# Pinning the matmul order of a Sinkhorn mixture of experts, spreading the Sinkhorn calls, and keeping two Strassen sums in PSUM

## The chip, the core and the metric

The kernel runs on one core of a Trainium2 chip. The metric is the device time of one execution in microseconds (us). The profile names the engines PE (TensorE, matmuls; PEld is its weight load), DVE (VectorE), ACT (ScalarE), POOL (GpSimd) and SP (SyncE, which issues the DMAs). PSUM is the memory that TensorE writes its results to; the kernel uses it in eight banks.

## The reference

A banded attention feeds a dense mixture of experts. The attention has 4 batches, 8 heads, 768 positions and 64 columns a head; a position sees 8 global positions and the last 96. Its output, as x of 3072 tokens by 512 columns, goes through all 8 experts, and the experts' outputs are mixed with weights P that a Sinkhorn iteration balances:

```python
logits = x @ w_gate
P = np.exp(logits - logits.max())
for _ in range(8):
    P /= P.sum(1, keepdims=True) + 1e-09
    P /= P.sum(0, keepdims=True) + 1e-09
    P *= N / E
for e in range(E):                       # w1[e]: 512 x 1024, w2[e]: 1024 x 512
    h = np.maximum(x @ w1[e], 0.0)
    out += P[:, e:e + 1] * (h @ w2[e])
```

Everything is float32.

## The kernel before

Each float32 operand of the mixture is split into a high and a low part (`hh`/`hl`, `w2h`/`w2l` and so on), and a product takes three matmuls: high by low, low by high, high by high.

The first 350 us or so are the attention, with part of expert 0 computed in its gaps (the filler). There the matmuls go through the class `InOrder`, which pins each of them behind the one traced before it on TensorE. After the attention, `moe.pe = nc.tensor` lifts the pinning. The last filler, the last gate and all of the mixture then run in whatever order the planner chose. The planner orders each engine's instructions ahead of time with a simulated timeline of its own; on the chip each engine works through its list in that order.

The mixture is a list of 120 steps, `steps`, in two halves of 60. A step is a pair of 128-column blocks of hidden units of one expert (`g`) for 768 tokens (`b`). Two neighbouring steps mostly share the weights of one `g` and take the two token blocks of the half. A step has two parts:

- The first layer, `layer1_strassen` (L641 on): x times w1 for two blocks by two, as seven Strassen products of six matmuls each, 42 in all, each 384 columns wide. The products accumulate in four PSUM banks, `c`, `d`, `a`, `b`, in the order m3 (c), m2 (d), m1 (a), m6 (b), m5 (c), m4 (d), m7 (a). ACT copies bank c to `t3` after m3 (L657); DVE forms the other sums (L659 to L670) in the two SBUF tiles `t3` and `h22`. `relu_split` then makes `hh` on ACT (L624) and `hl` on DVE (L625) from `h22`, `c`, `d` and `t3`. There are four such banks (`mps`), so each step uses the banks of the step before again.
- The second layer, `second`: six output tiles `y_ps` of 128 tokens, each of six matmuls 512 columns wide (L684 to L686), 36 in all, in three PSUM buffers (`yps`). DVE evicts each tile into the accumulator `acc`, times a column of P (L936); for expert 0, which is not scaled yet, it only adds (L932). At the first tiles of expert 1, ACT scales what expert 0 left in `acc` (L935).

The trace of the program goes: first layer of step n, weight split for the next g (`strassen_pair`: casts on ACT at L536, differences on POOL at L537), second layer of step n - 1.

P is computed by the generator `sinkhorn`, which `second` advances with `next`. It takes eleven calls: the first two find the maximum, the third takes exp and the first row sums, each later one does a matmul with ones for the column sums (`c_ps`, L747), the column division (L749 to L753) and, except in the last, the next row division (L741 to L744). With three calls a second layer it ends within the first four, all of which belong to expert 0.

Of the kernel before, what the change touches and what calls it, by code (L numbers as in the profile page):

```python
# [12 lines left out]
ALU = mybir.AluOpType  # L13
# [480 lines left out]
class Moe:  # L494
# [146 lines left out]
    def layer1_strassen(self, x, w, hpool, tmp, ps, tag):  # L641

        nc, KH = self.nc, self.KH
        wh, wl = w[0:2]
        left = {"m1": 0, "m2": 1, "m3": 5, "m4": 6, "m5": 2, "m6": 3, "m7": 4}
        bank = {n: ps.tile([P, UNIT], F32, name=f"bank_{n}", tag=tag) for n in "cdab"}

        def product(m, n, first, last):
            i, (xh, xl) = left[m], x[m]
            self.products(bank[n], lambda c: wh[:, i, c], lambda c: wl[:, i, c], lambda c: xh[:, c],  # L650
                          lambda c: xl[:, c], KH, first, last)

        a, b, c, d = (bank[n] for n in "abcd")
        tt = nc.vector.tensor_tensor
        product("m3", "c", True, False)
        t3 = tmp.tile([P, UNIT], F32, name="t3")
        nc.scalar.copy(out=t3, in_=c)  # L657
        product("m2", "d", True, False)
        tt(out=t3, in0=t3, in1=d, op=ALU.subtract)  # L659
        product("m1", "a", True, False)  # L660
        h22 = tmp.tile([P, UNIT], F32, name="h22")
        tt(out=h22, in0=a, in1=t3, op=ALU.add)
        product("m6", "b", True, True)
        tt(out=h22, in0=b, in1=h22, op=ALU.add)  # L664
        product("m5", "c", False, True)
        product("m4", "d", False, True)
        tt(out=t3, in0=d, in1=t3, op=ALU.add)
        tt(out=t3, in0=t3, in1=c, op=ALU.subtract)
        product("m7", "a", False, True)
        tt(out=t3, in0=a, in1=t3, op=ALU.add)  # L670
        r22 = self.relu_split(h22, hpool)
        r12 = self.relu_split(c, hpool)
        r21 = self.relu_split(d, hpool)
        r11 = self.relu_split(t3, hpool)
        return [r11, r21], [r12, r22]

    def layer2(self, t, w, hs, ps, tag):
# [78 lines left out]
def pipeline(tc, attention, ident, moe, acc):  # L756
# [6 lines left out]
    with ExitStack() as top:  # L763
# [72 lines left out]
        def differences(b, units=(0, 1)):  # L836
            for i in units:
                moe.right_difference(ops[b], i, xtmp, b == NB - 1)
            spill_blocks(b, ((0, KH), (1, 0)))
            settled.add(b)  # L840
# [49 lines left out]
        hpool = top.enter_context(tc.tile_pool(name="hpool", bufs=8, reuse_waits="tile"))  # L890
        tmp = top.enter_context(tc.tile_pool(name="ctmp", bufs=2, reuse_waits="tile"))

        def reload(b, pool):
            xs[2 * b], xs[2 * b + 1] = x_tiles(), x_tiles()
            new = [(pool.tile([P, KH, UNIT], F32R, name=f"sh{n}"), pool.tile([P, KH, UNIT], F32R, name=f"sl{n}"))
                   for n in range(3)]
            for i in range(2):
                for s in range(2):
                    nc.sync.dma_start(out=xs[2 * b + i][s].bitcast(F32), in_=x_spill[b][i][s].bitcast(F32))
            for i in range(3):  # L900
                for s in range(2):
                    nc.sync.dma_start(out=new[i][s].bitcast(F32), in_=s_spill[b][i][s].bitcast(F32))
            (h0, l0), (h1, l1) = xs[2 * b], xs[2 * b + 1]
            ops[b] = {"m1": new[0], "m2": (h0[:, 0:KH], l0[:, 0:KH]), "m3": (h1[:, 0:KH], l1[:, 0:KH]),
                      "m4": (h0[:, KH:], l0[:, KH:]), "m5": (h1[:, KH:], l1[:, KH:]), "m6": new[1], "m7": new[2]}
# [10 lines left out]
        def seed(b):  # L916
            for i in range(2):
                if 2 * b + i < NU - 1:
                    nc.sync.dma_start(out=acc_of[b][:, i * UT:(i + 1) * UT], in_=y_spill[2 * b + i])

        def second(g, b, hs):
            e = groups[g % NG][0]
            first_scaled = e != 0 and groups[g % NG - 1][0] == 0
            for i in range(2):
                for t in range(UT):
                    tt = (2 * b + i) * UT + t
                    y_ps = moe.layer2(t, wts[g], hs[i], yps, "y")
                    if t == 0 or i * t == 2:
                        next(sinkhorn, None)
                    a = acc_of[b][:, i * UT + t]  # L930
                    if e == 0:
                        nc.vector.tensor_tensor(out=a, in0=y_ps, in1=a, op=ALU.add)  # L932
                    else:
                        if first_scaled:
                            nc.scalar.mul(a, a, moe.pm[:, tt, 0:1])  # L935
                        nc.vector.scalar_tensor_tensor(out=a, in0=y_ps, scalar=moe.pm[:, tt, e:e + 1], in1=a,  # L936
                                                       op0=ALU.mult, op1=ALU.add)
                    if g % NG == NG - 1:
                        nc.sync.dma_start(out=moe.out[tt * P:(tt + 1) * P, :], in_=a)
# [2 lines left out]
            seed(b)  # L942
        sinkhorn = moe.sinkhorn(sps, "s")
        prev = None
        for n, (g, b) in enumerate(steps):
            hs = moe.layer1_strassen(ops[b], wts[g], hpool, tmp, mps, "h")
            if n == 0:
                with tc.issue_after(moe.latest.ins):
                    differences(NB - 1)
            for p, bs in enumerate(halves[:-1]):  # L950
                if b in bs and n == last_use[b]:
                    reload(halves[p + 1][bs.index(b)], sums[bs.index(b)])
            if g + 1 < 2 * NG and g + 1 not in wts:
                wts[g + 1] = moe.strassen_pair(moe.strassen_stage(*groups[(g + 1) % NG], stage), wpools[(g + 1) % 2])
            if prev is not None:
                second(*prev)
                for p, bs in enumerate(halves[:-1]):
                    if prev[1] in bs and n - 1 == last_use[prev[1]]:
                        seed(halves[p + 1][bs.index(prev[1])])
            prev = (g, b, hs)  # L960
        second(*prev)


@with_exitstack
def kernel(
# [31 lines left out]
    with tc.If(rv > 0) as cmp:  # L997
        pipeline(tc, band, ident, moe, acc)
    with cmp.Else():
        pipeline(tc, Dense(tc, q, k, v, ng, nl), ident, moe, acc)  # L1000
# [32 lines left out]
```

## Time and profile before

| | |
|---|---|
| time of three runs | 2261.06, 2262.77, 2263.44 us (median 2262.77) |
| the profiled execution's own time | 2260.31 us |
| its span, first to last instruction | 2258.5 us |
| granted TensorE clock | 0.996 of full |
| PE / DVE / ACT / POOL busy | 98% / 66% / 32% / 36% of the span |
| first mixture step starts | 368.9 us |

The profiled execution's time is its span and 1.8 us around it, and it lies 2.5 us under the median. Matmuls are pipelined: a matmul's row in the timeline shows a duration of 0.33 or 0.39 us, but the next one starts after about half of that, so it is the distance between starts that counts, and a TensorE that is "100% busy" can still be slower or faster. In a row of a group the numbers behind the bar are the busy time in us, the mean of one in ns, the idle time of the engine before it and what ended that.

### The profile page before, as it was taken

What the parts mean: (1) busy time and instruction counts of PE and PEld (TensorE: products, weight loads), DVE (VectorE), ACT (ScalarE), POOL (GpSimd) and SP (SyncE); (2) the same over time, 40 slices, a digit from 0 to 9 for tenths busy, and PEclk for the clock granted to TensorE, in tenths of its full rate; (3) what the DMA queues carried; (4) which work ended last, traced back from release to release, by engine and by line L of the source; (5) the groups of instructions that cost most, each with busy time, mean ns of one, the idle gap of its engine ahead of it and who ended that gap; (6) DMA issues with size and microseconds to landing.
All of it is one profiled execution on the core that took longest, in us unless ns stands there. A gap on an engine that the chain in (4) does not pass through costs nothing.

```text
span 2258.5 us, 31464 instructions
## 1 busy us (share of the span) xinstructions
PE 2224.2 (98%) x12147; PEld 1981.0 (88%) x12147; DVE 1501.7 (66%) x2682; ACT 712.9 (32%) x1592; POOL 819.5 (36%) x655
## 2 busy tenths in 40 slices
PE   7999999999999999999999999999999999999998
PEld 5788888989899898998999989989899898998997
DVE  5555457876666676666766666676676666766665
ACT  5676663232222222222222133222222222222221
POOL 4166366333333333333333234333333333333320
PEclk8999999999999999999999999999999999999999
DMA  6465432011100111001110451101111010111101
GB/s 167 121 178 160 127 102 66 29 38 38 38 28 29 38 38 38 28 29 38 38 38 29 166 206 39 38 29 34 32 38 38 29 38 29 38 38 31 36 19 58
DMA packets 177615, 133.74 MB, mean 59 GB/s; under 512 B 117041, under 2 KB 148785, under 8 KB 177457
## 3 DMA queue, kind: packets, MB, share of 16 engines
q1 hardware_dynamic: 177456, 131.65, 19.3%
q8 instruction: 97, 1.59, 0.3%
q14 instruction: 62, 0.50, 0.1%
HBM read 108.81 MB, written 22.81 MB: 58 GB/s over the span
## 4 chain that ended last, share of the span: by engine, by line
PE 91%; ACT 3%; DVE 2%; issue 2%; POOL 1%; DMA 0%; SPq 0%; ACTq 0%; DVEq 0%; POOLq 0%
PE y_ps L685 15%; PE y_ps L686 15%; PE y_ps L684 15%; PE bank_d L617 4%; PE bank_d L616 4%; PE bank_c L616 4%; PE bank_c L618 4%; PE bank_a L617 4%; PE bank_c L617 4%; PE bank_d L618 4%; PE bank_a L616 4%; PE bank_a L618 4%; PE bank_b L616 2%; PE bank_b L618 2%; PE bank_b L617 2%
## 5 line engine op out<-in xcount | busy, mean ns | idle before, releaser
L936 DVE SCALAR_TENSOR_TENSOR acc<-y_ps,pm,acc 128x512 f32<-128x512 f32 x672 | 499.9, 747 | 327.3 <-PE y_ps L686 324.7
L686 PE MATMUL y_ps<-w2h,hh 128*128 128x512 f32 x1440 | 567.5, 394 | 0.0
L685 PE MATMUL y_ps<-w2h,hl 128*128 128x512 f32 x1440 | 566.9, 394 | 0.0
L684 PE MATMUL y_ps<-w2l,hh 128*128 128x512 f32 x1440 | 561.8, 390 | 0.0
L537 POOL TENSOR_TENSOR w2l<-w2f,w2h 128x1024 fp32r<-128x1024 f32 x60 | 144.7, 2412 | 700.5 <-ACT w2h L536 700.5
L686 PEld LDWEIGHTS y_ps<-w2h,hh 128*128 128x128 f32 x1440 | 270.1, 188 | 53.7
L684 PEld LDWEIGHTS y_ps<-w2l,hh 128*128 128x128 f32 x1440 | 270.4, 188 | 43.5 <-DVE acc L936 0.2
L685 PEld LDWEIGHTS y_ps<-w2h,hl 128*128 128x128 f32 x1440 | 270.0, 188 | 43.4
L559 POOL TENSOR_TENSOR wsum<-w1f 128x256 f32<-128x256 f32 x300 | 223.6, 781 | 219.1 <-DMA w1f<-in_moe_w_dram 219.1
L537 POOL TENSOR_TENSOR wl<-wsum,wh 128x1280 fp32r<-128x1280 f32 x60 | 177.6, 2959 | 281.1 <-ACT wh L536 281.1
L624 ACT ACTIVATE hh<-h 128x384 fp32r<-128x384 f32 x120 | 63.1, 526 | 501.1 <-DVE h L664 499.6
L625 DVE SCALAR_TENSOR_TENSOR hl<-t,hh 128x384 fp32r<-128x384 f32 x120 | 165.4, 1378 | 9.9 <-ACT hh L624 9.8
L616 PE MATMUL bank_c<-xl,wh 128*128 128x384 f32 x480 | 162.0, 337 | 1.6 <-ACT t L657 1.6
L616 PE MATMUL bank_d<-xl,wh 128*128 128x384 f32 x480 | 160.9, 335 | 1.7 <-DVE t L670 1.7
L618 PE MATMUL bank_c<-xh,wh 128*128 128x384 f32 x480 | 161.9, 337 | 0.0
L617 PE MATMUL bank_c<-xh,wl 128*128 128x384 f32 x480 | 161.2, 336 | 0.0
L617 PE MATMUL bank_d<-xh,wl 128*128 128x384 f32 x480 | 161.2, 336 | 0.0
L617 PE MATMUL bank_a<-sh,wl 128*128 128x384 f32 x480 | 161.1, 336 | 0.0
L616 PE MATMUL bank_a<-sl,wh 128*128 128x384 f32 x480 | 161.0, 336 | 0.0
L618 PE MATMUL bank_a<-sh,wh 128*128 128x384 f32 x480 | 160.8, 335 | 0.0
L618 PE MATMUL bank_d<-xh,wh 128*128 128x384 f32 x480 | 160.3, 334 | 0.0
L625 DVE SCALAR_TENSOR_TENSOR hl<-h,hh 128x384 fp32r<-128x384 f32 x120 | 111.2, 927 | 68.7 <-ACT hh L624 68.7
(195 smaller groups left out, 3891.7 us busy)
## 6 DMA issues: line engine op xcount, KB each, us to landing
w1f<-in_moe_w_dram SPq DMA_DIRECT2D x62, 512.0 KB, 3.4
w2f<-in_moe_w_dram SPq DMA_DIRECT2D x62, 512.0 KB, 3.7
out_dram<-acc SPq DMA_DIRECT2D x24, 256.0 KB, 2.2
ys<-y_sb SPq DMA_DIRECT2D x21, 256.0 KB, 2.6
acc<-ys SPq DMA_DIRECT2D x7, 768.0 KB, 4.4
acc<-in_q_dram SPq DMA_DIRECT2D x32, 96.0 KB, 2.7
acc<-in_k_dram SPq DMA_DIRECT2D x32, 96.0 KB, 2.6
acc<-in_v_dram SPq DMA_DIRECT2D x32, 96.0 KB, 2.2
```

What stands on the lines that cost most here:

```text
L537: self.nc.gpsimd.tensor_tensor(out=lo, in0=full, in1=hi, op=ALU.subtract)
L559: nc.gpsimd.tensor_tensor(out=s[:, n], in0=x, in1=y, op=op)
L616: self.pe.matmul(out, lhsT=hi(c), rhs=xlo(c), start=(first and c == 0), stop=False, skip_group_check=True)
L617: self.pe.matmul(out, lhsT=lo(c), rhs=xhi(c), start=False, stop=False, skip_group_check=True)
L618: self.pe.matmul(out, lhsT=hi(c), rhs=xhi(c), start=False, stop=(last and c == n - 1), skip_group_check=True)
L624: nc.scalar.activation(out=hh, in_=src, func=AF.Relu)
L625: self.latest = nc.vector.scalar_tensor_tensor(out=hl, in0=src, scalar=0.0, in1=hh, op0=ALU.max, op1=ALU.subtract)
L684: self.pe.matmul(y_ps, lhsT=hh[:, cols], rhs=lf, start=(f == 0), stop=False)
L685: self.pe.matmul(y_ps, lhsT=hl[:, cols], rhs=wf, start=False, stop=False)
L686: self.pe.matmul(y_ps, lhsT=hh[:, cols], rhs=wf, start=False, stop=(f == n - 1))
L936: nc.vector.scalar_tensor_tensor(out=a, in0=y_ps, scalar=moe.pm[:, tt, e:e + 1], in1=a, op0=ALU.mult, op1=ALU.add)
```

## The change

```diff
@@ layer1_strassen
         h22 = tmp.tile([P, UNIT], F32, name="h22")
         tt(out=h22, in0=a, in1=t3, op=ALU.add)
         product("m6", "b", True, True)
-        tt(out=h22, in0=b, in1=h22, op=ALU.add)
+        tt(out=b, in0=b, in1=h22, op=ALU.add)
         product("m5", "c", False, True)
         product("m4", "d", False, True)
         tt(out=t3, in0=d, in1=t3, op=ALU.add)
         tt(out=t3, in0=t3, in1=c, op=ALU.subtract)
         product("m7", "a", False, True)
-        tt(out=t3, in0=a, in1=t3, op=ALU.add)
-        r22 = self.relu_split(h22, hpool)
+        tt(out=a, in0=a, in1=t3, op=ALU.add)
+        r22 = self.relu_split(b, hpool)
         r12 = self.relu_split(c, hpool)
         r21 = self.relu_split(d, hpool)
-        r11 = self.relu_split(t3, hpool)
+        r11 = self.relu_split(a, hpool)
@@ second, in pipeline
                     y_ps = moe.layer2(t, wts[g], hs[i], yps, "y")
-                    if t == 0 or i * t == 2:
+                    if i + t == 0:
                         next(sinkhorn, None)
@@ pipeline, before the loop over steps
         sinkhorn = moe.sinkhorn(sps, "s")
         prev = None
+        moe.pe = attention.pe
         for n, (g, b) in enumerate(steps):
```

Three things change. The last sums for h22 and h11 are written back into the banks b and a, and `relu_split` reads them from there. `next(sinkhorn)` is called once a second layer, after the matmuls of its first tile, instead of three times (after the first tile of each half and the last tile of the second). And the matmuls of the steps, with those of the Sinkhorn iteration, are pinned in the order in which the program traces them; the last filler and gate, traced before, are not.

With one call a second layer the iteration ends in the eleventh of them. The second layers 4 to 9 (counted from 0), which scale with P, therefore use a P after 2 to 7 of its 8 column divisions.

## The prediction

> **What bounds the kernel now.** First the engines' busy times, then the same over the long run of mixture steps (columns: PE, PEld, DVE, ACT, POOL with instructions, granted clock, DMA).
>
> ```profile
> span 2258.5 us, 31464 instructions
> PE 2224.2 (98%) x12147; PEld 1981.0 (88%) x12147; DVE 1501.7 (66%) x2682; ACT 712.9 (32%) x1592; POOL 819.5 (36%) x655
> ```
>
> ```profile
> 480.00:2230.00 1750.00, 1750.00 (x8725) 1575.72 (x8725) 1193.71 (x1790) 431.24 (x790) 588.02 (x491) 1.00 0.13 44
> ```
>
> TensorE never stops for 1750 us and its clock is full. A step has 42 first-layer matmuls (384 columns) and 36 second-layer ones (512 columns), 78 in all, so 8725 matmuls are 111.9 steps of 15.645 us. Every other engine has slack. A gain can therefore come only from the distance between matmul starts. Is that distance fixed? The timeline of TensorE, long runs of one kind first:
>
> ```profile
> 354.43 0.33 PE L618 MATMUL h_ps<-xh,w1h 128*128 128x384 f32 x1
> ...
> 359.63 0.33 PE L618 MATMUL h_ps<-xh,w1h 128*128 128x384 f32 x1
> ...
> 2242.12 0.39 PE L686 MATMUL y_ps<-w2h,hh 128*128 128x512 f32 x1
> ...
> 2251.64 0.39 PE L686 MATMUL y_ps<-w2h,hh 128*128 128x512 f32 x1
> ```
>
> Thirty starts take 5.20 us: 0.1733 us per 384-column matmul. Forty-two take 9.52 us: 0.2267 us per 512-column one. Now a stretch of a normal step, where the planner mixes the two kinds:
>
> ```profile
> 906.02 0.39 PE L684 MATMUL y_ps<-w2l,hh 128*128 128x512 f32 x1
> ...
> 907.41 0.33 PE L616 MATMUL bank_a<-sl,wh 128*128 128x384 f32 x1
> ...
> 908.45 0.39 PE L684 MATMUL y_ps<-w2l,hh 128*128 128x512 f32 x1
> ...
> 911.21 0.33 PE L616 MATMUL bank_c<-xl,wh 128*128 128x384 f32 x1
> ...
> 912.28 0.39 PE L684 MATMUL y_ps<-w2l,hh 128*128 128x512 f32 x1
> ```
>
> Six wide ones take 1.39 us instead of 6 x 0.2267 = 1.36 (0.03 over), and the six narrow ones behind them 1.04 (nothing over). Twelve wide ones take 2.76 instead of 2.72 (0.04 over), and the six narrow ones behind those 1.07 instead of 1.04 (0.03 over). Changing the kind costs 0.03 us a pair of runs where the wide run is short, 0.07 where it is long, and no more after that: the first matmuls of a run are dear, the later ones are at the bare distance.
>
> **The order (traced order pinned on TensorE).** Bare, a step is 42 x 0.1733 + 36 x 0.2267 = 15.440 us. It takes 15.645, so 0.205 us a step are lost, though nothing waits. Over the 1750 us the timeline changes kind 556 times each way, 4.97 pairs a step, 0.041 a pair, which lies between the two prices above. After the change a step has one pair, of the long sort: 0.07. Over 120 steps: 24.6 us before, 8.4 after, **-16.2 us**. No other operation is added or removed on TensorE.
>
> What covered waits until now was the freedom to take another matmul; that cover goes. I go through a step by hand, from the start of a first-layer block: seven products of 6 x 0.1733 = 1.04 us. Product 5 adds into bank c at 4.16 and needs ACT's copy of c, possible at 1.3 to 1.8. Product 7 needs h22, which DVE has at about 4.0, against 6.24. The last relu and split end about 2 us into the second-layer block, which lasts 8.2 us. A y tile takes 1.37 us there; the first can be evicted (0.75, row below) by 2.8, and its buffer, one of three, is wanted for the fourth tile at 4.1. So no wait in a normal step; the tightest margin is that 1.3 us.
>
> **The two sums in PSUM.** Groups by line, with shapes kept apart:
>
> ```profile
> L936 DVE SCALAR_TENSOR_TENSOR acc<-y_ps,pm,acc 128x512 f32<-128x512 f32 x672 | 499.9, 747 | 327.3 <-PE y_ps L686 324.7 <-ACT acc L935 0.3
> L625 DVE SCALAR_TENSOR_TENSOR hl<-t,hh 128x384 fp32r<-128x384 f32 x120 | 165.4, 1378 | 9.9 <-ACT hh L624 9.8
> L625 DVE SCALAR_TENSOR_TENSOR hl<-h,hh 128x384 fp32r<-128x384 f32 x120 | 111.2, 927 | 68.7 <-ACT hh L624 68.7
> L664 DVE TENSOR_TENSOR h<-bank_b,h 128x384 f32<-128x384 f32 x120 | 66.7, 556 | 48.8 <-PE bank_b L618 48.4
> L625 DVE SCALAR_TENSOR_TENSOR hl<-bank_c,hh 128x384 fp32r<-128x384 f32 x120 | 66.2, 552 | 31.0 <-ACT hh L624 31.0
> L624 ACT ACTIVATE hh<-bank_c 128x384 fp32r<-128x384 f32 x120 | 59.0, 491 | 266.4 <-DVE t L668 266.2 <-PE y_ps L686 0.2
> L381 DVE TENSOR_TENSOR o_ps<-o_ps,inv 128x384 f32<-128x384 f32 x32 | 17.9, 561 | 2.8 <-PE o_ps L83 2.8
> L935 ACT ACTIVATE acc<-acc,pm 128x512 f32<-128x512 f32 x24 | 16.0, 716 | 11.5 <-DVE acc L932 9.1 <-DVE pm L753 2.4
> ```
>
> A sum written back to PSUM costs what it did (561 against 556 ns). The splits of h22 and t3, 927 and 1378 ns, should fall to the 552 of a split from a bank: 120 x (0.375 + 0.826) = 144 us less of DVE. All of it is off the path: **0**, since DVE has 34% idle. In return banks a and b stay occupied until the split, some 1.6 us longer; free about 2 us into the second-layer block, they are wanted again at 8.2 + 2.1 (a) and 8.2 + 3.1 (b). Without this relief the last split would end 0.8 us later and the margin of 1.3 us would be 0.5.
>
> **Sinkhorn, one call a step.** There are eleven calls. Before, three a second-layer block finish P in the first four blocks, which only add expert 0 and do not read P. After, block k (from 0) makes call k+1, so blocks 4 to 10 read a P that is written between their first tile's matmuls and that tile's eviction. The matmul order is pinned, so the fourth tile waits for the first tile's buffer. Rows of one call now (TensorE, then DVE), and a slow one:
>
> ```profile
> 427.55 0.49 PE L747 MATMUL c_ps<-pm,ones 128*128 128x192 f32 x2
> 427.73 0.53 PE L684 MATMUL y_ps<-w2l,hh 128*128 128x512 f32 x1
> 428.10 0.40 PE L685 MATMUL y_ps<-w2h,hl 128*128 128x512 f32 x1
> ```
>
> ```profile
> 412.55 0.35 DVE L741 TENSOR_REDUCE rsum<-pm 128x24 f32<-128x192 f32 x1
> 412.93 0.18 DVE L742 TENSOR_SCALAR rsum<-rsum 128x24 f32<-128x24 f32 x1
> ...
> 413.62 0.29 DVE L743 RECIPROCAL rsum<-rsum 128x24 f32<-128x24 f32 x1
> 413.95 0.36 DVE L744 TENSOR_TENSOR pm<-pm,rsum 128x192 f32<-128x192 f32 x1
> ...
> 428.07 0.36 DVE L749 TENSOR_REDUCE csum<-c_ps 128x8 f32<-128x192 f32 x1 [0.33 <-PE c_ps L747]
> ...
> 429.11 0.36 DVE L753 TENSOR_TENSOR pm<-pm,csum 128x192 f32<-128x192 f32 x1
> ...
> 459.39 0.35 DVE L749 TENSOR_REDUCE csum<-c_ps 128x8 f32<-128x192 f32 x1
> ...
> 463.12 0.35 DVE L744 TENSOR_TENSOR pm<-pm,rsum 128x192 f32<-128x192 f32 x1
> ```
>
> From the c_ps matmul to the column sum 0.52 us, the column part 1.40 (428.07 to 429.47), the row part 1.18 in four operations plus 0.09 between them, the eviction 0.75, hand-overs about 0.15: 4.1 us. c_ps starts 1.39 us into the block, so the buffer comes free at 5.5. The fourth tile is due at 18 x 0.2267 + 0.04 + 0.32 (c_ps: 428.10 - 427.55 less one matmul) = 4.44. A wait of 1.1 us, and 1.9 in blocks 4 and 5, where ACT's scaling of acc (0.716) stands between. Block 10 has only the column part and does not wait. So 4 x 1.1 + 2 x 1.9 = 8.2 us at DVE's best. In the slow call the two parts took 463.47 - 459.39 = 4.08 instead of 2.67; all six like that would be 16.7. If DVE's queue found a way to hide it, 0. Nearest to the fast rows, with 0.4 a call for small operations that come out long: **+10.6 us**, ends 0 and 16.7. The call itself costs the same 0.32 us of TensorE wherever it stands.
>
> **The start.** The last filler and gate keep their freedom, so up to the first step nothing changes. Then TensorE now waits twice:
>
> ```profile
> 375.23 0.44 PE L616 MATMUL bank_c<-xl,wh 128*128 128x384 f32 x1 [1.62 <-ACT t L657]
> ...
> 381.62 0.44 PE L616 MATMUL bank_d<-xl,wh 128*128 128x384 f32 x1 [1.43 <-DVE t L670]
> ```
>
> The first stays, with the max transpose moved out of it (0.3 longer). In traced order step 0 then ends at 375.23 + 3 x 1.04 + 0.1 = 378.45, and step 1's first product needs bank c: product 6 and its sum (0.55), the sum with c (0.55), relu (0.49), split (0.55), hand-overs: about 379.8. A wait of 1.35 in place of 1.43. **+0.3 us**, ends -1 and +3 (DVE is full here).
>
> **Sum.** -16.2 + 10.6 + 0.3 = -5.3 us, so a span of 2253.2, 2255.0 against this execution's own 2260.3. Its 2260.3 lies 2.5 under the median 2262.8; on the median's scale I predict 2257.5 us.
>
> **Rivals.** *The wait for P is hidden* (other work of the planner on DVE falls so that the chain starts early): -16.2 + 0.3, 2246.9 us. Against it: c_ps is pinned behind the first tile, and the 4.1 us of the chain's own operations are longer than the 3.05 between c_ps and the fourth tile.
>
> *The distance belongs to the matmul, not to the order*: each kind would keep its mean, and the 0.205 us a step would stay. Then only the waits are left: 2262.8 + 10.9 = 2273.7, slower. For it: no wait shows in the 0.205 us. Against it: the same lines run at the bare distance in long runs. The Trainium skill (TensorE: Matmul & The Clock Gate, section "Wait — 56ns, not 53.3ns?") has a rule of this sort: columns over 2.4 GHz and a fixed 2.5 ns per matmul, whatever the neighbours. By it the two distances would be 0.1625 and 0.2158 us; the trace disagrees with both (0.1733, 0.2267) and with the fixed cost, under which the order would be worth nothing and this rival's time would hold.
>
> *The pinned order meets ACT's casts, slower.* ACT works in order, and where a weight split stood before the copy of c, TensorE waited:
>
> ```profile
> 371.96 1.29 ACT L536 CAST wh<-wsum 128x1280 fp32r<-128x1280 f32 x1
> ...
> 374.68 0.50 ACT L657 COPY t<-bank_c 128x384 f32<-128x384 f32 x1
> ```
>
> The casts took 2.7 us here. If the planner put all of them ahead of the copy in each of the 60 weight pairs, the copy would end at 1.3 + 2.7 + 0.5 = 4.5 against 4.16, 0.35 late plus 0.1 of restart, 60 times: +27 us, 2284 with the rest. It decides from 2.4 us of ACT work ahead of the copy. Against it: the two large casts are released at different times, by the last first-layer matmul and by the last second-layer matmul on the old weights, 7 to 8 us apart.
>
> **How the numbers follow.** Main forecast 0.66, hidden wait 0.12, fixed distance 0.07, ACT's casts 0.10, 0.05 for what I don't see. The main forecast's own range, from the ends of its two unknown costs, is 2246 to 2266. It straddles 2258.3, which is 0.2% (4.5 us, about what a measurement here can tell from no change) under 2262.8: 0.34 faster, 0.30 the same, 0.02 slower. The hidden wait is faster, the next two rivals are slower, and the rest goes 0.01, 0.02, 0.02: faster 0.47, same 0.32, slower 0.21. Range 2247 to 2266.
>
> **What would show it.** In the timeline of TensorE runs of 42 and 36 matmuls, and from 600 us on a step of 15.51 us (15.645 - 0.135). Six waits of y_ps for DVE's acc, of 1 to 2 us, in the first 170 us of steps. DVE's busy time down by about 140 us, with both splits near 550 ns. I am wrong if TensorE waits for a bank or a y buffer in normal steps too, or if the runs are long and the distance does not fall.

## The result, and the profile after

The changed kernel takes 2277.34 us (four runs, 2276.79 to 2278.22), the kernel before on the same chip 2261.91: a ratio of 1.0068 with a 95% interval of 1.0053 to 1.0083. That is 15.4 us slower; 5.3 us faster was forecast.

The page gives the totals, and the busy times by stretch (PE, PEld, DVE, ACT, POOL, each with its instructions, then granted clock, DMA share and GB/s) show where they come from.

```profile
span 2275.4 us, 31412 instructions
PE 2221.9 (98%) x12147; PEld 1983.7 (87%) x12147; DVE 1393.7 (61%) x2682; ACT 693.3 (30%) x1592; POOL 793.8 (35%) x655
```

```profile
440.00:600.00 160.00, 139.86 (x656) 122.97 (x655) 103.86 (x199) 36.68 (x68) 40.90 (x36) 0.94 0.09 27
...
600.00:2230.00 1630.00, 1630.00 (x8200) 1477.97 (x8199) 1016.73 (x1682) 390.13 (x746) 533.08 (x464) 1.00 0.14 45
```

The long stretch of the kernel before, for comparison:

```profile
600.00:2230.00 1630.00, 1630.00 (x8132) 1468.34 (x8131) 1112.92 (x1666) 402.92 (x738) 546.86 (x455) 1.00 0.14 44
```

From 600 us on the forecast holds. 1630 us divided by 8200 matmuls, times 78, is a step of 15.505 us; before it was 15.634. Over 120 steps that is 15.5 us gained. The loss sits between 440 and 600 us, where TensorE is idle for 20 of 160 us and its granted clock is 0.94. TensorE's waits in the steps (us in total, times, longest) name the cause, and the timeline gives the seven waits of the first row one by one:

```profile
PE y_ps L83 <- DVE acc L936: 20.1, 7, 4.8
PE bank_c L83 <- ACT t L657: 1.9, 1, 1.9
PE y_ps L83 <- DVE acc L932: 1.2, 3, 0.5
PE bank_d L83 <- DVE hl L625: 0.3, 1, 0.3
```

```profile
462.09 0.80 PE L83 MATMUL y_ps<-w2l,hh 128*128 128x512 f32 x1 [4.82 <-DVE acc L936]
462.69 0.63 PE L83 MATMUL y_ps<-w2h,hl 128*128 128x512 f32 x1
463.11 0.63 PE L83 MATMUL y_ps<-w2h,hh 128*128 128x512 f32 x1
463.54 0.63 PE L83 MATMUL y_ps<-w2l,hh 128*128 128x512 f32 x1
...
482.64 0.50 PE L83 MATMUL y_ps<-w2l,hh 128*128 128x512 f32 x1 [1.99 <-DVE acc L936]
...
502.84 0.80 PE L83 MATMUL y_ps<-w2l,hh 128*128 128x512 f32 x1 [4.07 <-DVE acc L936]
522.76 0.50 PE L83 MATMUL y_ps<-w2l,hh 128*128 128x512 f32 x1 [1.23 <-DVE acc L936]
542.95 0.80 PE L83 MATMUL y_ps<-w2l,hh 128*128 128x512 f32 x1 [4.06 <-DVE acc L936]
561.68 0.50 PE L83 MATMUL y_ps<-w2l,hh 128*128 128x512 f32 x1 [1.24 <-DVE acc L936]
580.56 0.79 PE L83 MATMUL y_ps<-w2l,hh 128*128 128x512 f32 x1 [2.73 <-DVE acc L936]
```

The number in brackets is the idle time ahead of the instruction. These are blocks 4 to 10, in order. Two things strike. The waits alternate: 1.99, 1.23 and 1.24 us are about what the forecast had (1.9 and 1.1), but every other one is some 2.8 us longer, and block 10, for which no wait was forecast, waits 2.73. And behind a long wait the matmuls start every 0.427 us instead of 0.227. The clock granted there was half:

```profile
462.00:467.00 5.00, 4.91 (x12) 3.84 (x13) 2.11 (x4) 2.32 (x4) 3.50 (x5) 0.50 0.00 0
483.00:488.00 5.00, 5.00 (x25) 4.32 (x24) 3.16 (x5) 2.77 (x5) 0.00 (x0) 1.00 0.00 0
```

DVE's timeline in block 4 shows why the long waits are long, beside the one POOL instruction that runs at that time:

```profile
454.58 0.36 DVE L749 TENSOR_REDUCE csum<-c_ps 128x8 f32<-128x192 f32 x1 [0.94 <-PE c_ps L83]
454.97 2.27 DVE L750 TENSOR_SCALAR csum<-csum 128x8 f32<-128x8 f32 x1
...
457.40 0.51 DVE L625 SCALAR_TENSOR_TENSOR hl<-bank_c,hh 128x384 fp32r<-128x384 f32 x1
...
457.89 0.55 DVE L625 SCALAR_TENSOR_TENSOR hl<-bank_d,hh 128x384 fp32r<-128x384 f32 x1
458.36 0.55 DVE L625 SCALAR_TENSOR_TENSOR hl<-bank_a,hh 128x384 fp32r<-128x384 f32 x1
...
460.14 0.36 DVE L744 TENSOR_TENSOR pm<-pm,rsum 128x192 f32<-128x192 f32 x1
```

```profile
454.26 2.96 POOL L537 TENSOR_TENSOR wl<-wsum,wh 128x1280 fp32r<-128x1280 f32 x1 [5.18 <-ACT wh L536]
```

An operation on eight columns takes 2.27 us; in block 5 the same one takes 0.17. It ends at 457.24, and POOL's weight difference ends at 457.22. Weights are split every second step, so every second block is hit. The three splits that were late behind it then stand inside the chain. From the column sum to the end of L744 it is 5.92 us here and 2.73 in block 5.

### The profile page after: what moved, and what is told of

Read it like the earlier page. It is cut to its first block, busy times and chain, and to the rows that moved or that the text cites. A ratio compares the mean times of both kernels' runs of the same rounds, so it can differ in the third digit from the quotient of the medians.

```text
span 2275.4 us, 31412 instructions
## 1 busy us (share of the span) xinstructions
PE 2221.9 (98%) x12147; PEld 1983.7 (87%) x12147; DVE 1393.7 (61%) x2682; ACT 693.3 (30%) x1592; POOL 793.8 (35%) x655
## 4 chain that ended last, share of the span: by engine, by line
PE 88%; DVE 4%; POOL 3%; ACT 3%; issue 3%; DMA 0%; SPq 0%; ACTq 0%; POOLq 0%; DVEq 0%
PE y_ps L83 44%; PE bank_c L83 11%; PE bank_d L83 11%; PE bank_a L83 11%; PE bank_b L83 5%; PE h_ps L83 1%; ACT p_sb L291 1%; PE s_ps L83 1%; PE o_ps L83 1%; PE t_ps L86 1%; PE tp L86 1%; DVE hl L625 1%; POOL wsum L559 1%; POOL xres L600 0%; DVE csum L750 0%
## 5 line engine op out<-in xcount | busy, mean ns | idle before, releaser
L936 DVE SCALAR_TENSOR_TENSOR acc<-y_ps,pm,acc 128x512 f32<-128x512 f32 x672 | 502.1, 749 | 264.4 <-PE y_ps L83 262.6
L83 PE MATMUL y_ps<-w2l,hh 128*128 128x512 f32 x1524 | 602.3, 395 | 21.3 <-DVE acc L936 20.1
L83 PE MATMUL y_ps<-w2h,hh 128*128 128x512 f32 x1524 | 598.7, 393 | 0.0
L83 PE MATMUL y_ps<-w2h,hl 128*128 128x512 f32 x1524 | 598.2, 393 | 0.0
L83 PEld LDWEIGHTS y_ps<-w2l,hh 128*128 128x128 f32 x1524 | 288.4, 189 | 80.9 <-DVE acc L936 23.1
L83 PEld LDWEIGHTS y_ps<-w2h,hh 128*128 128x128 f32 x1524 | 287.6, 189 | 60.9
L83 PEld LDWEIGHTS y_ps<-w2h,hl 128*128 128x128 f32 x1524 | 288.2, 189 | 55.5
L536 ACT CAST w2h<-w2f 128x1024 fp32r<-128x1024 f32 x60 | 63.3, 1056 | 382.6 <-PE y_ps L83 373.5
L624 ACT ACTIVATE hh<-bank_b 128x384 fp32r<-128x384 f32 x120 | 59.1, 492 | 390.8 <-DVE bank_b L664 390.8
L657 ACT COPY t<-bank_c 128x384 f32<-128x384 f32 x120 | 57.8, 482 | 389.4 <-PE bank_c L83 388.9
L659 DVE TENSOR_TENSOR t<-t,bank_d 128x384 f32<-128x384 f32 x120 | 66.5, 554 | 170.9 <-PE bank_d L83 165.3
```

The source lines that it names most:

```text
L83: return self.tc.keep_in_program_order(self.engine.matmul(*args, **kw))
L536: self.nc.scalar.copy(out=hi, in_=full)
L624: nc.scalar.activation(out=hh, in_=src, func=AF.Relu)
```

## The experiments

The theory was: what the pinned order gains is real; the loss is the chain of P, lengthened in every second block by POOL's weight difference and by the queue on DVE, with the half clock behind the long waits on top. The rivals: the pinned order itself costs in the early steps; or the sums in PSUM do; or the queue on DVE does it all. The kernels that keep one call a block read the unfinished P that the change reads, unless another place of the call is given.

**The call moved to the last tile** (order pinned, sums in PSUM). The scaled second layers read a P that is not finished here too.

```diff
-                    if i + t == 0:
+                    if i * t == 2:
                         next(sinkhorn, None)
```

> The changed kernel with its one Sinkhorn call a step moved from the first tile of the second layer to the last one (blocks 4 to 9 then scale with a P of 1 to 7 column divisions). Behind the last tile come 7.3 us of first layer that need no y buffer. Theory W: all waits of y_ps for acc are gone, the clock stays full, and what is left is the gain of the order: 2245 to 2249 us, a TensorE of 0.99 to 1.00 between 380 and 600 us. Rival O: 2270 to 2280 us.

2246.98 us, 0.9935 of before (0.9918 to 0.9951): 30.4 us faster than the change, and the fastest kernel here. The eviction that depends on the new P is now the last of its block, and a whole first layer follows before a y buffer is wanted. The list of TensorE's waits is that of the change without its first row, the other three rows unchanged. The same two stretches:

```profile
440.00:600.00 160.00, 160.00 (x808) 145.16 (x808) 122.72 (x231) 43.32 (x82) 51.93 (x45) 1.00 0.11 34
...
600.00:2230.00 1630.00, 1630.00 (x8199) 1478.58 (x8198) 1016.87 (x1682) 386.70 (x742) 522.34 (x455) 1.00 0.14 45
```

No wait for L936 is left, and 808 matmuls start between 440 and 600 us instead of 656. At 0.199 us each (15.505/78) those 152 are 30.2 us: the whole difference lies in this window. 20.1 us of it are the waits, some 10 the half clock and the restarts. In the timeline of the change 38 matmuls behind the four long waits start 0.32 to 0.60 us after the one before, which is 8.0 us more than at 0.2267.

**Three calls a block, order pinned**, so that P is finished before it is read, as before the change.

```diff
-                    if i + t == 0:
+                    if t == 0 or i * t == 2:
```

> The changed kernel with the Sinkhorn iteration called three times a second layer again, so that P is finished in blocks 0 to 3, before any eviction reads it. Theory W (the changed kernel lost its time in the evictions of blocks 4 to 10, which wait for P, and in the slow clock after those waits): no y_ps matmul waits for an eviction that scales with P; in blocks 1 to 3 the c_ps matmuls wait for the row part of the call before, 1 to 2 us each, about 4 to 10 us in all; the rest keeps the 16 us of the order: 2250 to 2256 us. Rival O (the pinned order itself costs the time, wherever the calls stand): 2270 to 2280 us.

2266.89 us (1.0023; 1.0014 to 1.0033), between the two. TensorE's waits:

```profile
PE c_ps L83 <- DVE pm L744: 9.7, 4, 3.2
PE bank_c L83 <- ACT t L657: 5.4, 2, 3.3
```

From 480 us on nothing was lost (8805 matmuls start between 480 and 2230 us, 8804 with the call at the last tile). Three calls a block put the next call's own matmul behind DVE's chain, and in a pinned order everything stands behind that matmul. So the wait was moved, not removed. The forecast of 2250 to 2256 was a miss of the same kind as the main one: the c_ps waits came to 9.7 us, where 4 to 10 were expected, but the second wait for bank c (3.3 us) was not expected, and half clock behind some of the waits (0.92 in the mean from 400 to 440 us) was not counted.

**Three calls, order pinned only from the fifth step on.**

```diff
-        moe.pe = attention.pe
         for n, (g, b) in enumerate(steps):
+            if n == 5:
+                moe.pe = attention.pe
```

> Free order and three Sinkhorn calls for the first five steps, as in the kernel before; pinned order from step 5 on; both sums in PSUM. Theory W: nothing waits for P, and 115 of 120 steps get the 0.135 us of the long runs: 2262 - 15.5, that is 2245 to 2249 us, faster than both kernels. Rival O: 2268 to 2278 us, as the changed kernel in its 115 pinned steps.

2253.64 us (0.9964; 0.9951 to 0.9976): better, but 4.6 us over the upper end of what was expected, with two waits of 3.0 us left at the hand-over:

```profile
PE y_ps L83 <- DVE acc L936: 3.0, 1, 3.0
PE c_ps L747 <- DVE pm L744: 3.0, 1, 3.0
```

**The sums in PSUM alone**, on the kernel before:

```diff
-        tt(out=h22, in0=b, in1=h22, op=ALU.add)
+        tt(out=b, in0=b, in1=h22, op=ALU.add)
...
-        tt(out=t3, in0=a, in1=t3, op=ALU.add)
-        r22 = self.relu_split(h22, hpool)
+        tt(out=a, in0=a, in1=t3, op=ALU.add)
+        r22 = self.relu_split(b, hpool)
...
-        r11 = self.relu_split(t3, hpool)
+        r11 = self.relu_split(a, hpool)
```

> The kernel before with the two sums in PSUM alone (free order, three calls). Theory: DVE's splits fall to 0.55 us, its busy time by 100 to 140 us, none of it on the path: 2259 to 2264 us, the same. Rival (banks a and b held longer make TensorE wait): 2266 us or more.

**One call a block alone**, on the kernel before with its free order:

```diff
-                    if t == 0 or i * t == 2:
+                    if i + t == 0:
```

> The kernel before with one Sinkhorn call a second layer alone (free order, sums in SBUF; blocks 4 to 9 scale with a P of 2 to 7 column divisions). Theory W says that the wait for P costs only because TensorE may not take another matmul meanwhile: here it can, so 2260 to 2266 us. Rival (the call itself in blocks 4 to 10 is what costs, in any order): 2275 us or more.

The sums alone take 2262.1 us (1.0001; 0.9991 to 1.001), the one call alone 2261.03 us (0.9998; 0.9988 to 1.0007). Each part is worth nothing by itself. The one call a block costs its 30 us only where the order is pinned; in the free order other matmuls fill the time, though DVE was held up there too: in the one call alone an L750 took 2.27 us and an L752 2.61.

**The change without the sums in PSUM** (the four edits above taken back).

```diff
-        r22 = self.relu_split(b, hpool)
+        r22 = self.relu_split(h22, hpool)
...
-        r11 = self.relu_split(a, hpool)
+        r11 = self.relu_split(t3, hpool)
```

> The changed kernel with the two sums back in SBUF (pinned order, one call at the first tile). Theory: the sums matter only through DVE's queue in blocks 4 to 10, where splits stand in the chain; with the slower SBUF splits the waits grow by 0 to 2 us each: 2277 to 2290 us. Rival (the sums in PSUM are what made the changed kernel slow): 2265 us or less.

2278.81 us (1.0076; 1.006 to 1.0093), and the wait is the same:

```profile
PE y_ps L83 <- DVE acc L936: 20.5, 7, 4.9
```

So the sums neither caused the loss nor saved much from it.

**csum in PSUM.** If POOL's weight difference holds up the SBUF-to-SBUF operation L750, that operation should be short once csum lies in PSUM.

```diff
-            c_ps = ps.tile([P, TT, E], F32, name="c_ps", tag=tag)
+            c_ps = ps.tile([P, TT + 1, E], F32, name="c_ps", tag=tag)
...
-            csum = small.tile([P, E], F32, name="csum")
+            csum = c_ps[:, TT]
```

> The changed kernel with csum kept in the PSUM tile of c_ps instead of SBUF. In the changed kernel the second operation on csum (L750) took 2.27 us in blocks 4, 6, 8 and 10, while POOL's weight difference was running, and 0.17 in the others. Theory L (the long operation is DVE held up by POOL at SBUF): L750 takes 0.2 us or less in every block, the four long waits shrink by about 2 us each to 2.0 to 3.0, and the half clock behind them mostly goes: 2260 to 2268 us. Rival Q (the wait is long because of the splits that the planner queued between, or for anything else on DVE): L750 stays long or another operation takes its place, 2273 to 2279 us.

2290.93 us (1.0129; 1.0113 to 1.0146). All eight L750 became short, and the wait fell from 20.1 to 12.6 us. Yet the kernel got slower, in all of the later steps, where 2260 to 2268 us had been expected:

```profile
L750 DVE TENSOR_SCALAR c_ps<-c_ps x8: 165/174/175, 441.2 to 571.2; 128x8 f32<-128x8 f32 x8
```

```profile
600.00:2230.00 1630.00, 1630.00 (x8096) 1460.80 (x8095) 1006.17 (x1662) 385.41 (x739) 529.77 (x463) 1.00 0.14 44
```

That is a step of 15.704 us, 24 us over 120 steps, at full clock and with the order unchanged. Only one thing else differed. Without csum every later tile on the left side of SBUF lies 32 bytes lower: in the changed kernel the tiles of x, `hh` and `hl` start at multiples of 64 bytes, here 32 past one. Three kernels asked whether that is it.

**csum in PSUM, with an unused tile of 32 bytes in csum's old place.**

```diff
+            if _ == 0:
+                nc.gpsimd.memset(small.tile([P, E], F32, name="pad"), 0.0)
             csum = c_ps[:, TT]
```

> The csum-in-PSUM kernel again, with one unused SBUF tile of 32 bytes a partition in the place that csum left, so that every later SBUF tile lies where it lies in the changed kernel. Theory A (where the operands lie made the steady step longer): the step goes back to 15.50 us, 120 x 0.21 = 25 us less than the 2290.9 of the kernel without the unused tile; 2262 to 2268 us, with the waits for acc at 12 to 13 us. Rival B (csum in PSUM itself lengthens the steps): the step stays at 15.71, 2288 to 2293 us.

2268.35 us (1.003; 1.0019 to 1.0042), 22.6 us less for one unused tile, and 0.35 over the upper end of what was expected.

```profile
600.00:2230.00 1630.00, 1630.00 (x8202) 1478.12 (x8201) 1017.36 (x1683) 389.25 (x747) 530.48 (x463) 1.00 0.14 44
```

```profile
PE y_ps L83 <- DVE acc L938: 13.0, 7, 3.1
```

```profile
457.07 0.17 DVE L752 TENSOR_SCALAR c_ps<-c_ps 128x8 f32<-128x8 f32 x1
```

```profile
456.35 2.96 POOL L537 TENSOR_TENSOR wl<-wsum,wh 128x1280 fp32r<-128x1280 f32 x1 [5.19 <-ACT wh L536]
```

The step is back at 15.501. The operation that took 2.27 us (L752 in this kernel) takes 0.17 in the middle of POOL's 2.96. So the hold-up is shown, and with the same addresses its removal is worth 7.1 us of waits and 9.0 us of time. Block 10 now waits 0.7 us; blocks 4, 6 and 8 still wait 3.1, 2.4 and 2.4, with the splits inside the chain. So the 20.1 us of the change come apart by these two kernels: about 9 are the chain at DVE's best (2.0 in blocks 4 and 5, 1.25 in 6 to 9), 7.1 the hold-up, and the other 4 what is left in blocks 4, 6, 8 and 10 above that. The timeline puts those 4 down to the splits; no kernel here takes them out of the chain.

**The change with the addresses shifted.** First all left-side tiles behind `gm`, by putting `gm` and `gmax` into one tile; then only `hh`, `hl` and the two SBUF sums, with an unused tile ahead of their pools.

```diff
-        gm = small.tile([P, 1], F32, name="gm")
+        both = small.tile([P, 2], F32, name="both")
+        gm, gmax = both[:, 0:1], both[0:1, 1:2]
...
-        gmax = small.tile([1, 1], F32, name="gmax")
```

```diff
+        hpad = top.enter_context(tc.tile_pool(name="hpad", bufs=1))
+        nc.gpsimd.memset(hpad.tile([P, E], F32, name="pad"), 0.0)
         hpool = top.enter_context(tc.tile_pool(name="hpool", bufs=8, reuse_waits="tile"))
```

> The changed kernel with the two one-column tiles gm and gmax put into one tile, which moves every later SBUF tile on the left side 32 bytes down and does nothing else. Theory A: the step becomes 15.71 us, 120 x 0.21 = 25 us more, 2299 to 2306 us. Rival B: the addresses do not matter, 15.50 and 2275 to 2280 us.

> The changed kernel with an unused tile of 32 bytes a partition ahead of the pool of hh and hl (and of the sums t3 and h22), so that of the matmuls' operands only the stationary hh and hl of the second layer move by 32 bytes. Theory H (the stationary operand's place decides): the distance of the second-layer matmuls goes from 228 to 233 ns, 36 x 5 = 0.18 us a step, 2295 to 2301 us. Rival X (the moving operand's place decides, here only x of the first layer, which does not move): step 15.50, 2275 to 2280 us.

2301.37 us (1.0177; 1.016 to 1.0194) and 2300.53 us (1.0173; 1.0156 to 1.019): 24.0 and 23.2 us over the change. The piece of the chain that is one second layer, first in the change, then with `hh` and `hl` shifted (start, us, what):

```profile
640.08 8.20 PE y_ps L83 x36
```

```profile
644.95 8.40 PE y_ps L83 x36
```

0.20 us a second layer, 24 us over 120. In the shifted kernel a long run does not settle: from the first to the second of these rows of its timeline there are 19 starts in 4.43 us, 0.233 each, where the long run before had 0.2267.

```profile
899.72 0.40 PE L83 MATMUL y_ps<-w2h,hl 128*128 128x512 f32 x1
...
904.15 0.40 PE L83 MATMUL y_ps<-w2h,hh 128*128 128x512 f32 x1
```

The place of the stationary operands `hh` and `hl` accounts for all of it (the two SBUF sums that move with them are read by no matmul); x, which moves too in the first of the two, adds nothing that can be told apart.

**Idle matmuls in blocks 4, 6, 8 and 10** (twelve 512-column ones into an unused PSUM tile, ahead of the fourth tile), to keep the clock up.

```diff
+                    if k in (4, 6, 8, 10) and i == 0 and t == 2:
+                        w_ps = sps.tile([P, DM], F32, name="w_ps", tag="s")
+                        for m in range(12):
+                            moe.pe.matmul(w_ps, lhsT=hs[0][0][0][:, 0:P], rhs=wts[g][2][:, 0],
+                                          start=(m == 0), stop=(m == 11))
```

Here `k` is the number of the step, handed to `second` with the rest.

> The changed kernel with 12 matmuls of no use (512 columns, 2.7 us, into the free Sinkhorn bank) between the third and the fourth tile of blocks 4, 6, 8 and 10, where TensorE waits 2.9 to 5.0 us. Theory C (part of the loss is the granted clock, 0.5 after a wait of 3 us or more): the waits shrink by the 2.7 us and the matmuls behind them start every 0.227 instead of 0.427 us; about 8 us go: 2267 to 2271 us. Rival (the slow matmuls are slow for another reason, such as operands): 2276 to 2280 us.

2272.44 us (1.0045; 1.0028 to 1.0062): matmuls whose result nobody reads made the kernel 4.9 us faster (4.2 when both are set against the kernel before that ran beside them).

```profile
458.96 2.88 PE L83 MATMUL w_ps<-w2h,hh 128*128 128x512 f32 x12
463.95 0.50 PE L83 MATMUL y_ps<-w2l,hh 128*128 128x512 f32 x1 [2.11 <-DVE acc L936]
464.29 0.40 PE L83 MATMUL y_ps<-w2h,hl 128*128 128x512 f32 x1
464.52 0.39 PE L83 MATMUL y_ps<-w2h,hh 128*128 128x512 f32 x1
```

L750 still takes 2.27 us here and DVE's chain is as long; but the starts after the wait are 0.23 us apart, not 0.43. It is 1.4 us over the expected 2267 to 2271. Two things that work against it show. The 2.06 us wait for bank c at 377.35 us was followed by ten starts 0.32 us apart instead of 0.1733, some 1.6 us, where the 1.86 us wait in its place in the change was not. And the 2.03 us wait of block 5, which had no idle matmuls, was now followed by half clock, seen in the mean of this stretch:

```profile
480.00:500.00 20.00, 17.97 (x83) 15.90 (x83) 11.47 (x19) 8.81 (x15) 5.55 (x3) 0.91 0.08 27
```

**The pinned order with the kinds mixed.** The kernel with the call at the last tile, its first layer and second layer traced in turns, so that there are five changes of kind each way a step instead of one.

```diff
-            hs = moe.layer1_strassen(ops[b], wts[g], hpool, tmp, mps, "h")
+            first = moe.layer1_strassen(ops[b], wts[g], hpool, tmp, mps, "h")
+            tiles = iter(()) if prev is None else second(*prev)
...
+                next(tiles, None)
...
-                second(*prev)
+                for _ in tiles:
+                    pass
```

Here `first` yields after products 3 to 6 and returns `hs` after product 7; after each yield one tile of the second layer is traced, and the last two tiles when the first layer is done.

> The kernel with the call at the last tile and the order pinned, but with four of the six second-layer tiles traced between the first layer's products (three products, tile, product, tile, product, tile, product, tile, product, two tiles): five changes of kind each way a step instead of one, with nothing else different. Theory K (what the free order lost is the change of kind): 4 more pairs at 0.041 us are 0.16 us a step, 15.66 us, 120 x 0.16 = 20 us over 2247: 2262 to 2270 us. Rival F (the loss came from something else in the free order): 15.50 us and 2245 to 2250 us.

2261.52 us (1.0; 0.9991 to 1.001): 14.5 us of the gain are gone, and the kernel takes what the kernel before did.

```profile
600.00:2230.00 1630.00, 1630.00 (x8130) 1466.86 (x8129) 1002.71 (x1669) 396.87 (x738) 523.33 (x455) 1.00 0.14 45
```

8130 matmuls are a step of 15.638 us, against 15.634 before with its 4.97 pairs. The four added pairs cost 0.131 us a step, 0.033 each. No wait for a y buffer appears. So what pinning gains is the sorting, as forecast, and not the pinning. A change of kind is a change of width and of layer at once, and no run here tells the two apart.

## Why the prediction was wrong

**The order: right.** -16.2 us was forecast, with a step of 15.51 us. The step is 15.505, which is 15.5 us over 120 steps; the kernel without the waits is 14.9 us faster than before; and mixing the kinds again took 14.5 us back. The rival in which the distance belongs to the matmul alone has fallen: the same 78 matmuls a step took 15.505 or 15.638 us by their order only.

**The sums in PSUM: right**, 0 against a ratio of 1.0001 on the kernel before. Both splits fell to 550 to 560 ns as said:

```profile
L625 DVE SCALAR_TENSOR_TENSOR hl<-bank_b,hh 128x384 fp32r<-128x384 f32 x120 | 66.9, 557 | 72.9 <-ACT hh L624 72.9
L625 DVE SCALAR_TENSOR_TENSOR hl<-bank_a,hh 128x384 fp32r<-128x384 f32 x120 | 66.0, 550 | 0.0
```

DVE's busy time fell by 108 us rather than 140. Added up over its rows, its operations fell by 130 (others became a little longer); busy time counts overlapping operations once, and they overlap less now.

**The start: right in the sum, by luck.** The wait of bank c grew to 1.86 us, as forecast. The second one, forecast at 1.35, was only 0.27, and three waits of y_ps for the evictions of expert 0, which the prediction did not have, made 1.15 (the largest 0.54). Together that is 3.3 us against 3.05 before, +0.2 where +0.3 was forecast.

**Sinkhorn, one call a step: the step that failed.** It was priced at +10.6 us with ends 0 and 16.7. It measured +30.4, the distance between the change and the same kernel with the call at the last tile. Three parts of the working went wrong.

First, "0.4 a call for small operations that come out long". The chain at DVE's best was right: 1.99, 1.23 and 1.24 us where 1.9 and 1.1 were worked out. What went wrong is how much longer it can get. The slow call that the prediction showed, 4.08 against 2.67 us, was slow for two reasons, both on the timeline of the kernel before:

```profile
449.19 2.39 POOL L537 TENSOR_TENSOR w2l<-w2f,w2h 128x1024 fp32r<-128x1024 f32 x1 [11.33 <-ACT w2h L536]
```

```profile
450.08 1.53 DVE L750 TENSOR_SCALAR csum<-csum 128x8 f32<-128x8 f32 x1
...
459.77 0.32 DVE L750 TENSOR_SCALAR csum<-csum 128x8 f32<-128x8 f32 x1
...
460.37 0.42 DVE L752 TENSOR_SCALAR csum<-csum 128x8 f32<-128x8 f32 x1
460.70 0.54 DVE L659 TENSOR_TENSOR t<-t,bank_d 128x384 f32<-128x384 f32 x1
...
461.82 0.55 DVE L662 TENSOR_TENSOR h<-bank_a,t 128x384 f32<-128x384 f32 x1
...
462.70 0.49 DVE L664 TENSOR_TENSOR h<-bank_b,h 128x384 f32<-128x384 f32 x1
```

About 1.0 of its 1.41 us are three sums of the first layer that stood between its operations. The other 0.4 are L750 and L752, 0.32 and 0.42 us instead of 0.17 each while POOL worked, and that is the surcharge that the sum took for every call. How long such a hold-up can be was there to see in the call before: L750 took 1.53 us and ended at 451.61, 0.03 after POOL's instruction. In the changed kernel POOL's weight difference comes back every second step, and in the pinned order it met the chain at its worst: 2.1 us from L750 and 1.1 from the splits behind it, 3.2 where 1.41 was the worst case. The Trainium skill (SBUF — State Buffer, section "Who interferes with whom") says that DVE's `tensor_scalar` in its two-port mode and a GpSimd instruction share one pair of ports, and that the later of the two is blocked until the earlier has finished. The trace agrees: L750 ended 0.02 us after POOL's instruction, and took 0.17 us under the same POOL instruction once its operands lay in PSUM. In which mode L750 ran the trace does not show.

Second, "block 10 has only the column part and does not wait". It waited 2.73 us, since L750 is in the column part. With that, the seven waits came to 20.1 us, 3.4 over the upper end.

Third, the price of a wait was taken to be its length. Behind the four long waits TensorE ran at half clock for 2.7 to 5.6 us, which costs 8.0 us; with the restarts and the like that is the other 10 us. No rival held it either. The Trainium skill (TensorE: Matmul & The Clock Gate, section "What's actually happening") has a clock that is halved after an idle window of about 3.4 us and comes back after a busy one. The 0.427 us starts at a granted 0.50 agree with the half rate. The lengths agree only in part: a wait of 2.73 us was followed by half clock in the change and one of 2.03 us in the kernel with idle matmuls. A wait of 1.99 us was not in the change and was in the kernel without the sums in PSUM, and the 3.34 us wait for bank c with three calls a block was not. So the length of a wait alone does not decide it, and what does no run here shows.

The rival on the other side, ACT's casts ahead of the copy of c, did not occur: no step after 600 us waits for anything.

## What to carry to other kernels

A pinned order paid here because it sorts the matmuls by kind, and it makes every late operand a stop for all of TensorE: put a small serial chain where its result is read last, not where it is produced first. A slow instance is to be taken apart into its causes before it is averaged, and every instance of the operation looked at, above all when a cause is periodic. And a test that frees or adds a small tile also moves what lies behind it: compare the addresses, or leave an unused tile in its place.

## What the hardware showed that was not expected

- The second layer's matmuls take 0.2267 us apart in a long run when their stationary operand starts at a multiple of 64 bytes, and 0.233 when it starts 32 bytes past one: 23 us of 2277 from an unused 32-byte tile. Why, no run here shows.
- A wait of about 2 us on TensorE can be followed by 3 us or so at half clock, and a wait of the same length or a longer one need not be: 1.99 us was in one kernel and not in another, and one of 3.34 us was not. Idle matmuls that covered most of each wait kept the clock behind it, and were worth 4 to 5 us net.
- A DVE operation on eight columns of SBUF took 2.27 us when it was issued 0.7 us after a POOL instruction of 2.96 us, and 0.17 under such an instruction with its operands in PSUM.
- Changing between the first layer's 384-column matmuls and the second's of 512 costs 0.033 us a pair of runs, with nothing waiting: 14.5 us here for four more pairs a step.
